# p'w_in of four batches made in one packing, on 64-row tiles, and kept in DRAM

## The chip, the core and the metric

The kernel runs on one core of a Trainium2 chip. The core has TensorE (PE in the profile, with its weight loads as PEld), VectorE (DVE), ScalarE (ACT), GpSimd (POOL) and SyncE (SP, which only issues DMAs here). The metric is the device time of one launch in microseconds (us).

## The reference

Two attentions in a row, and a feed-forward network (FFN) on top, for 8 batches of 8 heads, 576 tokens, head size 64, with 32 packed queries p:

```python
p_packed = sm_attn(p, k, v)                 # 32 rows a head
out = sm_attn(q, p_packed, p_packed)        # 576 rows a head
x = out.transpose(0, 2, 1, 3).reshape(4608, 512)
h = x @ w_in                                # 512 -> 2048
g = np.maximum(h, 0) + alpha * np.minimum(h, 0)
return g @ w_out                            # 2048 -> 512
```

sm_attn(a, k, v) is softmax(a kᵀ / 8) v. Inputs are float32 (w_in and w_out come as 64-bit floats).

## The kernel before, in words

**No x is made.** The second attention's weights a (576 x 32 a head) are multiplied with p'w_in, where p' is p_packed: for a batch, h = sum over heads of a · (p' w_in). p'w_in has 8 heads x 32 = 256 rows and 2048 columns a batch. Heads go in pairs: four pairs (pr), each of 128 rows of w_in.

**Two-part numbers.** Nearly every product is made from a rounded high part and the rest (hi and lo, `fp32r` in the profile), in three matmuls: hi·hi, lo·hi, hi·lo. A split is an ACT copy (hi) and a subtraction on DVE or POOL (lo).

**Stages, by the names in the profile.** `attention(b, tp)` does half a batch (two pairs): scores of p with k (L216, L217; evacuated by L219 and L220), softmax (L280 to L302), its transposes (L328, evacuated and split by L332, L334), v split (L308, L309, into the single buffer vs), the pack matmuls (L350; L358, L359), p' transposed (L375) and stored in two parts (L384, L385; POOL copies it to pt, L409). Then the scores of q with p' (L216, L217 again, with p as weights), and the softmax over 32 (L453 to L470), which leaves a_h and a_l. `packed_w` makes p'w_in of two batches: per column block j of 512 and pair pr, a unit, it reads a split tile of w_in from DRAM (w_split, L582), makes three matmuls of 128x512 with the p' of both batches as weights (L610 to L612) into one PSUM buffer of the two called ps_m, and copies it into pw by ACT (L615, once a batch). The FFN goes by half batches k (0 to 15) and 16 blocks f of 128 hidden columns: `first(k, f)` splits 256 columns of pw (`split_pw`, ACT L626, POOL L628), makes six matmuls of 288 columns (L652 to L654), and applies the activation (L658, L659) and the split (L664, L665); `second(k, f)` adds to four output accumulators in twelve matmuls (L682 to L684). A pair (k, f) is called a step here; steps are numbered 0 to 255 in the order of the list `order`. Batches 2 and 3 are steps 64 to 127, batches 4 and 5 128 to 191, batches 6 and 7 192 to 255.

**What sets the order.** The loop at the program's end writes the FFN step by step and advances the generators in `plan` (attention, packing) by one piece a step, from a given step on. A scheduler then orders each engine's instructions by its own model of time; each engine does its own in that order. All DMAs but two are issued by SP, in one order, each waiting for what it needs; the landings are counted on eight semaphores in turn, and a DMA first waits for the last one on its own semaphore. Before, attention of batches 2g, 2g+1 and their packing stand among the FFN steps of the two batches ahead of them.

**Buffers the change meets.** ps_m has 2 PSUM buffers, `win` (tiles of w_in) 3, `pwp` (pw) 8 of [128, 2, 512], `pt` one tile.

Of the kernel before, what the change touches and what calls it, by code (L numbers as in the profile page):

```python
# [28 lines left out]
def pack_attention_ffn_kernel(  # L29
# [20 lines left out]
    nc = tc.nc  # L50
# [43 lines left out]
    pt = const.tile([P, NP, 2, 2, 64], F32R, name="pt")  # L94
# [134 lines left out]
    def attention(b, tp, exact=False):  # L229
# [92 lines left out]
        for t0 in range(0, KT, 3):  # L322
# [10 lines left out]
            if not exact:  # L333
                nc.vector.tensor_tensor(  # L334
                    out=aT[:, ks, :, 1, :], in0=psq, in1=fv(aT[:, ks, :, 0, :]), op=ALU.subtract
                )
        q0 = load_x(qT, b, pr0)
        yield
        c = sm.tile([P, 2, P], F32, name="c", tag="c", bufs=2)

# [19 lines left out]

        pack(0, vs)
        vs = split_v(1)
        q1 = load_x(qT, b, pr1)
        yield
        pack(1, vs)
        q0 = split(q0)
# [9 lines left out]
        for r in range(2):  # L376
            rs, cs = slice(r * 64, r * 64 + 64), slice(r * N, r * N + N)
            if b == 0:
                for i, pr in enumerate(prs):
                    nc.scalar.copy(out=pt0[rs, pr, pr % 2, cs], in_=ppv[rs, i, cs])  # L380
            elif exact:
                nc.scalar.copy(out=ptf[rs, ts, b, cs], in_=ppv[rs, :, cs])
            else:
                nc.scalar.copy(out=p2[rs, ts, 0, cs], in_=ppv[rs, :, cs])  # L384
                nc.vector.tensor_tensor(  # L385
                    out=p2[rs, ts, 1, cs], in0=ppv[rs, :, cs], in1=fv(p2[rs, ts, 0, cs]),
                    op=ALU.subtract,
                )
        if exact:
            def split_pt():  # L390
                if b > 0:
                    nc.gpsimd.tensor_copy(out=pt[:, ts, 0, b, :], in_=ptf[:, ts, b])
                    nc.gpsimd.tensor_tensor(
                        out=pt[:, ts, 1, b, :], in0=ptf[:, ts, b], in1=fv(pt[:, ts, 0, b, :]),
                        op=ALU.subtract,
                    )
                    return
                for pr in prs:
                    nc.gpsimd.tensor_copy(out=pt[:, pr, 0, 0, :], in_=pt0[:, pr, pr % 2])
                    nc.gpsimd.tensor_tensor(  # L400
                        out=pt[:, pr, 1, 0, :], in0=pt0[:, pr, pr % 2], in1=fv(pt[:, pr, 0, 0, :]),
                        op=ALU.subtract,
                    )

            if b > 0:
                split_pt()
        else:
            for pr in prs:
                nc.gpsimd.tensor_copy(out=pt[:, pr, :, b % 2, :], in_=fv(p2[:, pr]))  # L409
        done.update(("p", b, pr) for pr in prs)  # L410
        owner.update({(pr, b % 2): b for pr in prs})
        q1 = split(q1)
        yield
        s2 = [] if b == 0 else wk.tile([P, S], F32, name="s2", tag="w")
# [203 lines left out]
            yield  # L618


    def split_pw(k, h):
# [4 lines left out]
        nc.scalar.copy(out=th, in_=src)  # L626
        low = nc.vector if k < 4 else nc.gpsimd
        low.tensor_tensor(out=tl, in0=src, in1=fv(th), op=ALU.subtract)  # L628
        pj[k, h] = (th, tl)

    def first(k, f):
        tok = slice((k % 2) * HS, (k % 2) * HS + HS)
        assert all(("a", k, tp) in done for tp in range(2)), ("a", k)
        assert k < 2 and ("wf", f) in done or all(("w", k // 2, f // 4, pr) in done for pr in range(4)), ("w", k, f)
        ps = ps_h.tile([P, 512], F32, name="ps_h", tag="h")
        if k < 2 * XF:
            th, a_f = pw[k // 2, f // 4], result[k // 2]
            fs = slice((f % 4) * P, (f % 4) * P + P)
            for i in range(2):
                nc.tensor.matmul(  # L640
                    ps[:, :HS], th[:, i, fs], a_f[:, i, tok], start=(i == 0), stop=(i == 1)
                )
        else:
            a_h, a_l = result[k // 2]
            key = (k, f // 2)
            if key not in pj:
                split_pw(*key)
            th, tl = pj[key]
            fs = slice((f % 2) * P, (f % 2) * P + P)
            for i in range(2):  # L650
                hi, lo = (i == 0), (i == 1)
                nc.tensor.matmul(ps[:, :HS], th[:, i, fs], a_h[:, i, tok], start=hi, stop=False)  # L652
                nc.tensor.matmul(ps[:, :HS], th[:, i, fs], a_l[:, i, tok], start=False, stop=False)  # L653
                nc.tensor.matmul(ps[:, :HS], tl[:, i, fs], a_h[:, i, tok], start=False, stop=lo)  # L654
# [3 lines left out]
        nc.scalar.activation(out=neg, in_=x, func=AF.Relu, scale=-1.0)  # L658
        nc.vector.scalar_tensor_tensor(  # L659
            out=x, in0=neg, scalar=nal[:, f : f + 1], in1=x, op0=ALU.mult, op1=ALU.add  # L660
        )
        gh = gp.tile([P, HS], F32R, name="gh", tag="gh", bufs=3)
        gl = gp.tile([P, HS], F32R, name="gl", tag="gl", bufs=3)
        nc.scalar.copy(out=gh, in_=x)  # L664
        nc.vector.tensor_tensor(out=gl, in0=x, in1=fv(gh), op=ALU.subtract)  # L665
        gs[k, f] = (gh, gl)
# [57 lines left out]
    def units(*js):  # L724
        return [(j, pr) for j in js for pr in range(NP)]
# [109 lines left out]
```

## Time and profile before

| | us |
|---|---|
| median of 3 runs | 800.36 (799.27 to 802.3) |
| profiled execution, its time | 800.34 |
| its span, first to last instruction | 798.5 |
| TensorE busy | 766.9 |
| ACT, DVE, POOL busy | 542.7, 501.1, 312.4 |
| first matmul of step 64, 128, 192 | 269.4, 458.2, 639.3 |
| packing matmuls of batches 4, 5 | 416.6 to 454.4 |
| packing matmuls of batches 6, 7 | 593.6 to 633.2 |

Rows of groups read: line, engine, operation, out<-in, shapes, count | busy us, mean ns of one | idle time before them and what ended it. Matmuls overlap, so a matmul's own time (0.3 us) is longer than the distance to the next. Rows of stretches give, for each engine, busy us and the number of instructions, then the granted TensorE clock, the mean busy share of the 16 DMA engines, and GB/s.

### The profile page before, as it was taken

The numbers are of one execution on the slowest core, as the hardware profiler recorded it, in microseconds if no ns is written. First come the engines' busy times: TensorE is split into PE (matmuls) and PEld (weight loads), VectorE is DVE, ScalarE is ACT, GpSimd is POOL, SyncE is SP. The second block draws the span as 40 slices with busy tenths as digits, with TensorE's granted clock in tenths as the row PEclk, the third lists the DMA queues.
The fourth block names the chain that finished last, engine by engine and source line by source line (L and its number), as shares of the span: only waits on it lengthen the run. The fifth ranks groups of instructions, "written<-read, shape, count | busy, mean of one in ns | idle before, by whom it ended". The sixth has DMA issues, their size and how long they took to land.

```text
span 798.5 us, 15192 instructions
## 1 busy us (share of the span) xinstructions
PE 766.9 (96%) x5376; PEld 729.6 (91%) x5376; DVE 501.1 (63%) x1112; ACT 542.7 (68%) x1260; POOL 312.4 (39%) x303
## 2 busy tenths in 40 slices
PE   5789997899999999999999999999999999999997
PEld 4566776799999999999999999999999999999997
DVE  4998998878978445666754365665763344444443
ACT  5778888876667977676768766776768644444443
POOL 2211211344535336675664145756543232222320
PEclk9989999999999999999999999999999999999999
DMA  9977896422234753222226621211017200000000
GB/s 333 291 258 256 268 337 219 129 76 60 90 94 126 252 180 92 76 60 75 64 80 219 214 71 50 89 49 58 1 54 253 68 31 1 31 1 31 1 31 30
DMA packets 58459, 93.79 MB, mean 117 GB/s; under 512 B 5136, under 2 KB 36880, under 8 KB 58384
## 3 DMA queue, kind: packets, MB, share of 16 engines
q1 hardware_dynamic: 58096, 92.75, 36.0%
q8 instruction: 42, 0.69, 0.3%
q14 instruction: 33, 0.27, 0.1%
q10 hardware_dynamic: 288, 0.07, 0.0%
HBM read 72.88 MB, written 19.92 MB: 116 GB/s over the span
## 4 chain that ended last, share of the span: by engine, by line
PE 78%; DVE 2%; ACT 1%; DMA 1%; issue 0%; ACTq 0%; DVEq 0%
PE acc L682 15%; PE acc L683 15%; PE acc L684 15%; PE ps_h L652 7%; PE ps_h L653 7%; PE ps_h L654 7%; PE ps_h L640 2%; PE ps_m L350 2%; PE ps_m L216 1%; PE ps_m L217 1%; PE ps_m L610 1%; PE ps_m L612 1%; PE ps_m L611 1%; PE ps_m L328 1%; DMA w<-w_split 1%; PE ps_m L375 0%
## 5 line engine op out<-in xcount | busy, mean ns | idle before, releaser
L682 PE MATMUL acc<-gh,wo 128*128 128x288 f32 x1024 | 287.2, 300 | 3.7 <-ACT gh L664 3.7
L683 PE MATMUL acc<-gh,wo 128*128 128x288 f32 x1024 | 282.8, 295 | 0.0
L659 DVE SCALAR_TENSOR_TENSOR ps_h<-neg,nal,ps_h 128x288 f32<-128x288 f32 x256 | 132.0, 517 | 141.0 <-ACT neg L658 140.1
L628 POOL TENSOR_TENSOR pwl<-pw,pwh 128x512 fp32r<-128x512 f32 x96 | 124.3, 1295 | 213.4 <-ACT pwh L626 192.1
L684 PE MATMUL acc<-gl,wo 128*128 128x288 f32 x1024 | 202.3, 300 | 0.0
L682 PEld LDWEIGHTS acc<-gh,wo 128*128 128x128 f32 x1024 | 192.3, 188 | 9.7 <-ACT gh L664 6.5
L683 PEld LDWEIGHTS acc<-gh,wo 128*128 128x128 f32 x1024 | 192.3, 188 | 1.7 <-issue 0.2
L665 DVE TENSOR_TENSOR gl<-ps_h,gh 128x288 fp32r<-128x288 f32 x256 | 115.8, 454 | 81.1 <-ACT gh L664 78.6
L684 PEld LDWEIGHTS acc<-gl,wo 128*128 128x128 f32 x1024 | 158.4, 188 | 4.2 <-issue 0.9
L664 ACT CAST gh<-ps_h 128x288 fp32r<-128x288 f32 x256 | 102.1, 400 | 79.5 <-DVE ps_h L659 77.8
L658 ACT ACTIVATE neg<-ps_h 128x288 f32<-128x288 f32 x256 | 104.7, 410 | 45.1 <-PE ps_h L654 39.3
L652 PE MATMUL ps_h<-a_h,pwh 128*128 128x288 f32 x448 | 133.2, 297 | 0.8 <-DVE gl L665 0.8
L653 PE MATMUL ps_h<-a_l,pwh 128*128 128x288 f32 x448 | 132.1, 295 | 0.0
L654 PE MATMUL ps_h<-a_h,pwl 128*128 128x288 f32 x448 | 132.1, 295 | 0.0
L626 ACT CAST pwh<-pw 128x512 fp32r<-128x512 f32 x112 | 69.4, 620 | 62.2 <-PE ps_h L653 60.9
L180 POOL TENSOR_TENSOR xl<-xraw,xh 128x576 fp32r<-128x576 f32 x48 | 69.0, 1440 | 93.0 <-ACT xh L179 88.8
L652 PEld LDWEIGHTS ps_h<-a_h,pwh 128*128 128x128 f32 x448 | 84.1, 188 | 2.0 <-DVE gl L665 1.6
L653 PEld LDWEIGHTS ps_h<-a_l,pwh 128*128 128x128 f32 x448 | 84.2, 188 | 0.4
L654 PEld LDWEIGHTS ps_h<-a_h,pwl 128*128 128x128 f32 x448 | 84.1, 188 | 0.2
L615 ACT COPY pw<-ps_m 64x512 f32<-64x512 f32 x120 | 69.6, 580 | 7.8 <-PE ps_m L612 5.7
L309 POOL TENSOR_TENSOR vs<-vraw,vs 128x640 fp32r<-128x640 f32 x24 | 38.1, 1586 | 32.4 <-ACT vs L308 32.3
L219 ACT COPY lo<-ps_m 64x288 f32<-64x288 f32 x96 | 37.2, 396 | 7.5 <-PE ps_m L217 5.8
(133 smaller groups left out, 996.2 us busy)
## 6 DMA issues: line engine op xcount, KB each, us to landing
w<-w_split SPq DMA_DIRECT2D x48, 512.0 KB, 4.2
xraw<-in_kT SPq DMA_DIRECT2D x32, 288.0 KB, 2.9
xraw<-in_qT SPq DMA_DIRECT2D x32, 288.0 KB, 2.9
outT<-ot SPq DMA_DIRECT2D x64, 144.0 KB, 2.3
vraw<-in_v SPq DMA_DIRECT2D x32, 256.0 KB, 2.9
wraw<-in_w_in SPq DMA_DIRECT2D x16, 512.0 KB, 4.8
wraw<-in_w_out SPq DMA_DIRECT2D x16, 512.0 KB, 4.9
w_split<-w SPq DMA_DIRECT2D x16, 512.0 KB, 4.1
```

The costliest lines, as they stand in the source:

```text
L615: nc.scalar.copy(out=pw[b, j][ro : ro + 64, pr // 2, :], in_=ps[i * 64 : i * 64 + 64, :])
L628: low.tensor_tensor(out=tl, in0=src, in1=fv(th), op=ALU.subtract)
L652: nc.tensor.matmul(ps[:, :HS], th[:, i, fs], a_h[:, i, tok], start=hi, stop=False)
L653: nc.tensor.matmul(ps[:, :HS], th[:, i, fs], a_l[:, i, tok], start=False, stop=False)
L654: nc.tensor.matmul(ps[:, :HS], tl[:, i, fs], a_h[:, i, tok], start=False, stop=lo)
L658: nc.scalar.activation(out=neg, in_=x, func=AF.Relu, scale=-1.0)
L659: nc.vector.scalar_tensor_tensor(out=x, in0=neg, scalar=nal[:, f : f + 1], in1=x, op0=ALU.mult, op1=ALU.add)
L664: nc.scalar.copy(out=gh, in_=x)
L665: nc.vector.tensor_tensor(out=gl, in0=x, in1=fv(gh), op=ALU.subtract)
L682: nc.tensor.matmul(acc[o][:, :HS], wo_t[f][:, 0, os_], gh, start=begin, stop=False)
L683: nc.tensor.matmul(acc[o][:, :HS], wo_t[f][:, 1, os_], gh, start=False, stop=False)
L684: nc.tensor.matmul(acc[o][:, :HS], wo_t[f][:, 0, os_], gl, start=False, stop=end)
```

## The change

For batches 0 to 3 nothing changes. For batches 4 to 7:

- Attention of all four is planned among steps 64 to 127 (`AG` has eight starts). For batches 6 and 7 it stops after p' (`HELD`), and the q part (load, split, scores) follows from steps 132 to 148 on.
- p' is kept in a tile `pt4`, which takes the place of `pt` and holds all four batches: each pair's tile has 128 columns, 32 rows of p' x 4 batches, and its upper 64 partitions belong to one head, its lower 64 to the other. POOL copies a held batch's p' back into `p2` for the scores of q.
- `packed_w_four` has 16 units as before, once in place of twice. A unit makes six matmuls with 64 rows and 128 columns of weights (three a head), each head into a ps_m buffer of its own. ACT copies each buffer into hi, DVE subtracts into lo, and two DMAs of 512 KB write hi and lo to a DRAM tensor `pw_four` (two-part p'w_in of four batches).
- `fetch_pw` reads the two parts for (k, j) back, 512 KB each, four steps ahead, into the same eight pwp tiles. The splits of pw (L626, L628) fall away for batches 4 to 7.

```diff
+    pw_four = [dram.tile([2, 2, P, 4, 512], F32, name=f"pw_four{j}") for j in range(NJ)]
...
+            while clock[0] < HELD[b][tp]:
+                yield
...
+    def packed_w_four(units):
+        def get(j, pr):
+            w = win.tile([P, 2, 512], F32R, name="w", tag="w")
+            nc.sync.dma_start(out=fv(w), in_=w_split[j, pr])
+            return w
...
+            ps = [ps_m.tile([P, 512], F32, name="ps_m", tag="m") for r in range(2)]
+            for n, (pp, wp) in enumerate(((0, 0), (1, 0), (0, 1))):
+                for r in range(2):
+                    rs = slice(r * 64, r * 64 + 64)
+                    nc.tensor.matmul(
+                        ps[r], pt_four()[rs, pr, pp], w[rs, wp], start=(n == 0), stop=(n == 2)
+                    )
+            hi, lo = (pwp.tile([P, 2, 512], F32R, name=n, tag="pw") for n in ("hi4", "lo4"))
+            for r in range(2):
+                nc.scalar.copy(out=hi[:, r], in_=ps[r])
+                nc.vector.tensor_tensor(out=lo[:, r], in0=ps[r], in1=fv(hi[:, r]), op=ALU.subtract)
+            for part, t in enumerate((hi, lo)):
+                to = pw_four[j][part, pr // 2, pr % 2 * 64 : pr % 2 * 64 + 64]
+                nc.sync.dma_start(
+                    out=to.rearrange("(r n) b c -> (n b) r c", r=2), in_=fv(t)
+                )
+            yield
+
+    def fetch_pw(k, j):
...
+        th, tl = (pwp.tile([P, 2, 512], F32R, name=n, tag="pw") for n in ("pwh4", "pwl4"))
+        for part, t in enumerate((th, tl)):
+            nc.sync.dma_start(
+                out=fv(t), in_=pw_four[j][part, :, :, k // 2 % 4].rearrange("t p c -> p t c")
+            )
+        pj[k, j] = (th, tl)
...
+    HELD = {6: (132, 136), 7: (144, 148)}
...
-    AG = (0, 4, 11, 17, 26)
+    AG = (0, 4, 9, 13, 18, 22, 27, 31, 39)
...
-    for g in range(2, B // 2):
-        T = (g - 1) * 4 * NF
-        plan += [(T + AG[n], attention(2 * g + n // 2, n % 2), 1) for n in range(4)]
-        plan += [(T + AG[4], packed_w([2 * g, 2 * g + 1], units(*range(NJ))), 1)]
+    T = 4 * NF
+    plan += [(T + AG[n], attention(4 + n // 2, n % 2), 1) for n in range(8)]
+    plan += [(T + AG[8], packed_w_four(units(*range(NJ))), 1)]
```

How the scheduler's order comes out is seen on TensorE and SP. On TensorE before, a unit of batches 4 and 5 (L610 to L612) stands in the middle of an FFN step of batches 2 and 3 (L684 and L682 to L683 are output matmuls of two steps that follow each other):

```order
L684 MATMUL acc_5801<-gl,wo_542 128x288
L684 MATMUL acc_5802<-gl,wo_542 128x288
L610 MATMUL ps_m<-w,pt 128x512
L611 MATMUL ps_m<-w,pt 128x512
L612 MATMUL ps_m<-w,pt 128x512
L684 MATMUL acc_5803<-gl,wo_542 128x288
L682 MATMUL acc_5800<-gh,wo_634 128x288
L683 MATMUL acc_5800<-gh,wo_634 128x288
```

After, all 96 matmuls of the 16 units (L671; pt_4025 is pt4) stand in one piece between the end of batch 7's p' (L224 and L225 scores, L359 pack, L386 p' transposed, L336 transposes) and the held scores of q (p_113 is p2):

```order
L359 MATMUL ps_m<-vs,aT 128x256 x5
L224 MATMUL ps_m<-xh,s_112 128x288
L225 MATMUL ps_m<-xl,s_112 128x288
L224 MATMUL ps_m<-xh,s_112 128x288
L225 MATMUL ps_m<-xl,s_112 128x288
L386 MATMUL ps_m<-ii,c 128x64 x2
L336 MATMUL ps_m<-ident,s_t 128x128 x5
L359 MATMUL ps_m<-vs,aT 128x256 x10
L386 MATMUL ps_m<-ii,c 128x64 x2
L671 MATMUL ps_m<-w,pt_4025 128x512 x96
L224 MATMUL ps_m<-xh,p_113 128x288
L225 MATMUL ps_m<-xl,p_113 128x288
```

The last output matmul of batches 2 and 3 (step 127) stands 16 rows ahead of L671, before the packs of the last two halves; the first FFN matmul of batch 4 (step 128) stands behind 14 of the held score matmuls. On SP, the first fetch for step 128 (L691) stands behind the writes (L680) of 15 of the 16 units:

```order
L657 DMA w<-w_split 128x1024
L680 DMA pw_four_104<-hi_6377 128x2x512
L680 DMA pw_four_104<-lo_6378 128x2x512
L680 DMA pw_four_104<-hi_6439 128x2x512
L680 DMA pw_four_104<-lo_6440 128x2x512
L680 DMA pw_four_104<-hi_6469 128x2x512
L680 DMA pw_four_104<-lo_6470 128x2x512
L691 DMA pwh_6631<-pw_four_101 128x2x512
L691 DMA pwl_6632<-pw_four_101 128x2x512
L680 DMA pw_four_104<-hi_6511 128x2x512
```

The earlier units have a read of w_split ahead of each pair of writes; the reads of the first three units stand far ahead, among the FFN steps.

More of the change, by code (lines that the diff above doesn't have):

```diff
@@ L93, in pack_attention_ffn_kernel @@
     p2 = const.tile([P, NP, 2, 64], F32R, name="p2")
[L94 removed]
+    pt = const.tile([P, NP, 2, 2, 64], F32R, name="pt", tag="pt")
     nc.gpsimd.memset(s1f, 0.0)
@@ L101, in pack_attention_ffn_kernel, with pt_four @@
     wo_t = {}
+    four = {}
+    def pt_four():
+        if not four:
+            four[0] = const.tile([P, NP, 2, P], F32R, name="pt4", tag="pt")
+        return four[0]
     XF = 1
@@ L336, in attention @@
                 )
-        q0 = load_x(qT, b, pr0)
+        if b not in HELD:
+            q0 = load_x(qT, b, pr0)
         yield
@@ L362, in attention @@
         vs = split_v(1)
-        q1 = load_x(qT, b, pr1)
+        if b not in HELD:
+            q1 = load_x(qT, b, pr1)
         yield
         pack(1, vs)
-        q0 = split(q0)
+        if b not in HELD:
+            q0 = split(q0)
         yield
@@ L383, in attention @@
             else:
[L384 to L388, printed above, removed]
+                if b in HELD:
+                    ph, pl = (pt_four()[rs, ts, part, b % 4 :: 4] for part in range(2))
+                else:
+                    ph, pl = (p2[rs, ts, part, cs] for part in range(2))
+                nc.scalar.copy(out=ph, in_=ppv[rs, :, cs])
+                nc.vector.tensor_tensor(out=pl, in0=ppv[rs, :, cs], in1=fv(ph), op=ALU.subtract)
         if exact:
@@ L406, in attention @@
                 split_pt()
-        else:
+        elif b < 4:
             for pr in prs:
                 nc.gpsimd.tensor_copy(out=pt[:, pr, :, b % 2, :], in_=fv(p2[:, pr]))
+        elif b not in HELD:
+            for r in range(2):
+                rs, cs = slice(r * 64, r * 64 + 64), slice(r * N, r * N + N)
+                for pr in prs:
+                    nc.gpsimd.tensor_copy(out=pt_four()[rs, pr, :, b % 4 :: 4], in_=fv(p2[rs, pr, :, cs]))
         done.update(("p", b, pr) for pr in prs)
         owner.update({(pr, b % 2): b for pr in prs})
+        if b in HELD:
+            while clock[0] < HELD[b][tp]:
+                yield
+            for r in range(2):
+                rs, cs = slice(r * 64, r * 64 + 64), slice(r * N, r * N + N)
+                for pr in prs:
+                    nc.gpsimd.tensor_copy(
+                        out=p2[rs, pr, :, cs], in_=fv(pt_four()[rs, pr, :, b % 4 :: 4])
+                    )
+            q0 = load_x(qT, b, pr0)
+            q1 = load_x(qT, b, pr1)
+            yield
+            q0 = split(q0)
+            yield
         q1 = split(q1)
@@ L618, in packed_w @@
             yield
+    def packed_w_four(units):
[3 more added lines that the diff above has]
+            return w
+        for got in ahead(get, units):
+            if got is None:
+                yield
+                continue
+            (j, pr), w = got
+            assert all(("p", b, pr) in done for b in range(4, 8)), pr
+            done.update(("w", b, j, pr) for b in range(4, 8))
+            ps = [ps_m.tile([P, 512], F32, name="ps_m", tag="m") for r in range(2)]
+            for n, (pp, wp) in enumerate(((0, 0), (1, 0), (0, 1))):
+                for r in range(2):
+                    rs = slice(r * 64, r * 64 + 64)
[3 more added lines that the diff above has]
+            hi, lo = (pwp.tile([P, 2, 512], F32R, name=n, tag="pw") for n in ("hi4", "lo4"))
+            for r in range(2):
+                nc.scalar.copy(out=hi[:, r], in_=ps[r])
[5 more added lines that the diff above has]
+                )
+            yield
+    def fetch_pw(k, j):
+        if (k, j) in pj or j == NJ:
+            return
+        assert all(("w", k // 2, j, pr) in done for pr in range(NP)), ("w", k, j)
+        th, tl = (pwp.tile([P, 2, 512], F32R, name=n, tag="pw") for n in ("pwh4", "pwl4"))
+        for part, t in enumerate((th, tl)):
+            nc.sync.dma_start(
+                out=fv(t), in_=pw_four[j][part, :, :, k // 2 % 4].rearrange("t p c -> p t c")
+            )
+        pj[k, j] = (th, tl)
     def split_pw(k, h):
@@ L644, in first @@
             a_h, a_l = result[k // 2]
-            key = (k, f // 2)
-            if key not in pj:
-                split_pw(*key)
+            if k < 8:
+                key = (k, f // 2)
+                if key not in pj:
+                    split_pw(*key)
+                fs = slice((f % 2) * P, (f % 2) * P + P)
+            else:
+                key = (k, f // 4)
+                fetch_pw(*key)
+                fs = slice((f % 4) * P, (f % 4) * P + P)
             th, tl = pj[key]
-            fs = slice((f % 2) * P, (f % 2) * P + P)
             for i in range(2):
@@ L783, in pack_attention_ffn_kernel @@
     plan += [(A2[4], packed_w([2, 3], units(*range(NJ))), 1)]
-    for g in range(2, B // 2):
-        T = (g - 1) * 4 * NF
-        plan += [(T + AG[n], attention(2 * g + n // 2, n % 2), 1) for n in range(4)]
-        plan += [(T + AG[4], packed_w([2 * g, 2 * g + 1], units(*range(NJ))), 1)]
-    AHEAD = 2
+    T = 4 * NF
+    plan += [(T + AG[n], attention(4 + n // 2, n % 2), 1) for n in range(8)]
+    plan += [(T + AG[8], packed_w_four(units(*range(NJ))), 1)]
+    AHEAD, FETCH = 2, 4
     for i in range(len(order) + AHEAD):
+        clock[0] = i
+        if i + FETCH < len(order) and order[i + FETCH][0] >= 8:
+            k, f = order[i + FETCH]
+            fetch_pw(k, f // 4)
         now = [gen for t, gen, n in plan for _ in range(max(1, -n)) if t <= i and (n < 0 or (i - t) % n == 0)]
```

1 line of the change is left out of this document (added).

## The prediction, made before the changed kernel ran

> **What bounds the kernel now.** I read the page's shares and its chain first, then the stretches by stage, then the places where the change acts.
>
> ```profile
> span 798.5 us, 15192 instructions
> PE 766.9 (96%) x5376; PEld 729.6 (91%) x5376; DVE 501.1 (63%) x1112; ACT 542.7 (68%) x1260; POOL 312.4 (39%) x303
> PE 78%; DVE 2%; ACT 1%; DMA 1%; issue 0%; ACTq 0%; DVEq 0%
> ...
> core 0: us, PE busy (x) PEld busy (x) DVE busy (x) ACT busy (x) POOL busy (x), PEclk, DMA share, GB/s
> 337.40:458.20 120.80, 120.48 (x880) 118.07 (x879) 67.28 (x152) 90.10 (x203) 63.90 (x59) 1.00 0.37 117
> 458.20:639.30 181.10, 181.10 (x1342) 178.88 (x1341) 103.04 (x236) 126.38 (x294) 90.02 (x80) 1.00 0.25 76
> 650.00:700.00 50.00, 50.00 (x380) 50.00 (x379) 21.22 (x44) 22.57 (x55) 12.92 (x10) 1.00 0.04 13
> ```
>
> TensorE is the bound: it is never idle in the two stretches where this change works. 380 matmuls in 50 us make 0.132 us each for the 288-wide ones, weight load included, although one lasts 0.3 us. The other engines have slack. So whatever empties TensorE's queue costs its full length, and nothing saved on ACT or POOL gains anything here.
>
> **Where the orders part.** TensorE's two orders are the same up to five pack matmuls behind the output matmuls of step 84:
>
> ```profile
> 336.27 0.69 PE L684 MATMUL acc<-gl,wo 128*128 128x288 f32 x4
> 336.80 0.76 PE L350 MATMUL ps_m<-vs,aT 128*128 128x256 f32 x5
> 337.39 0.33 PE L375 MATMUL ps_m<-ii,c 128*128 128x64 f32 x2
> 337.53 0.38 PE L682 MATMUL acc<-gh,wo 128*128 128x288 f32 x1
> ...
> 458.19 0.29 PE L652 MATMUL ps_h<-a_h,pwh 128*128 128x288 f32 x1
> ...
> 430.59 0.23 PE ps_m L611
> 430.82 0.23 PE ps_m L612
> ```
>
> So until 337.4 us nothing changes. 458.19 is the first matmul of step 128, that is of batch 4. Five pack matmuls take 0.59 us (0.118 each), two p' transposes 0.14 (0.07 each), and the last two rows, of the chain, price a 512-wide packing matmul at 0.23.
>
> **Before the block.** Counted in the two orders, up to the last output matmul of step 127 the changed kernel has, against the old one's way to 458.19: 48 packing matmuls fewer (48 x 0.23 = 11.0); 22 score matmuls more (2.9), 10 transposes (1.2, priced as the pack's), 20 pack (2.4), 4 p' (0.3) and 17 output matmuls (2.2). That is -2.0, so 456.2 us. ACT gains attention work here and loses 32 pw copies; its 90 us of 120.8 were covered by TensorE and stay so. I add no stall, but 0 to 6 in the range, as more of the attention is now chained.
>
> **The block.** In the order, TensorE then has nothing but this before step 128: transposes, packs, scores and p' of batch 7 (10 T, 20 pack, 8 score, 4 p', some 5 us of work), all 96 new packing matmuls in one piece, and 14 score matmuls of the held halves. TensorE issues in order, and no FFN step is left to fill the gaps. Its length is that of the chains. First the attention tail:
>
> ```profile
> L698 DVE COPY ot<-acc 128x288 f32<-128x288 f32 x24 | 9.9, 449 | 5.3 <-PE acc L684 5.2
> L280 DVE TENSOR_REDUCE nmx<-s_t 128x1 f32<-128x576 f32 x14 | 10.4, 745 | 0.2
> L294 ACT ACTIVATE s_t<-s_t,nmx 128x576 f32<-128x576 f32 x14 | 10.9, 777 | 0.5 <-DVE nmx L281 0.3
> L302 DVE TENSOR_SCALAR s_t<-s_t,den 128x576 f32<-128x576 f32 x12 | 7.1, 590 | 0.2
> L332 ACT CAST aT<-ps_m 128x384 fp32r<-128x384 f32 x12 | 5.8, 482 | 1.5 <-PE ps_m L328 1.4
> L334 DVE TENSOR_TENSOR aT<-ps_m,aT 128x384 fp32r<-128x384 f32 x12 | 6.6, 550 | 1.1 <-ACT aT L332 1.1
> L308 ACT CAST vs<-vraw 128x640 fp32r<-128x640 f32 x24 | 17.7, 737 | 0.0
> L309 POOL TENSOR_TENSOR vs<-vraw,vs 128x640 fp32r<-128x640 f32 x24 | 38.1, 1586 | 32.4 <-ACT vs L308 32.3
> L358 ACT COPY ct<-ps_m 128x128 f32<-128x128 f32 x24 | 6.5, 269 | 6.2 <-PE ps_m L350 5.9
> L219 ACT COPY lo<-ps_m 64x288 f32<-64x288 f32 x96 | 37.2, 396 | 7.5 <-PE ps_m L217 5.8
> L220 DVE TENSOR_TENSOR s_t<-ps_m,lo 64x288 f32<-64x288 f32 x48 | 21.2, 449 | 17.0 <-ACT lo L219 16.5
> L179 ACT CAST xh<-xraw 128x576 fp32r<-128x576 f32 x48 | 32.3, 673 | 5.4 <-PE ps_m L216 3.1 <-issue 1.3 <-DVE wo L142 1.0
> L385 DVE TENSOR_TENSOR p<-ps_m,p 64x64 fp32r<-64x64 f32 x24 | 5.2, 218 | 1.8 <-ACT p L384 1.3
> ```
>
> From the last output matmul: ot copy 0.45, max scaled and exponential 1.1, division 0.9, five transposes with their two-part split 2.4, pack 0.9: 5.8. The second pack waits for scores that stand ahead of it: ct 0.27, vs cast 0.74, lo 0.40, xh 0.67, lo 0.40, add 0.45, pack 0.9: 3.8. The scores of the last half: ct, vs, lo, xh, lo, add and a matmul's 0.3: 3.2. Its softmax: 0.75, 0.2, exponential 0.9, division 0.9, small copies 0.3: 3.0. Transposes and first pack 2.8. Second pack behind the single vs buffer: 0.27 + 0.74 + 1.59 + 0.9 = 3.5. p' and its four small copies: ct 0.27, add 0.3, a matmul's 0.4, 4 x 0.22: 1.9. Sum 24, with hand-overs **25**; bounds 20 (packs hidden) and 30.
>
> Then the packing. A unit fills both ps_m buffers, and each must be copied by ACT and subtracted by DVE before its next use:
>
> ```profile
> L610 PE MATMUL ps_m<-w,pt 128*128 128x512 f32 x56 | 22.4, 399 | 1.5 <-ACT w L141 1.0 <-DMA w<-w_split 0.6
> L626 ACT CAST pwh<-pw 128x512 fp32r<-128x512 f32 x112 | 69.4, 620 | 62.2 <-PE ps_h L653 60.9 <-POOL xl L180 0.9
> L588 DVE TENSOR_TENSOR w<-w,w 128x512 fp32r<-128x512 f32 x8 | 6.3, 789 | 0.4 <-ACT w L587 0.3
> ...
> w<-w_split SPq DMA_DIRECT2D x48, 512.0 KB, 4.2
> w_split<-w SPq DMA_DIRECT2D x16, 512.0 KB, 4.1
> outT<-ot SPq DMA_DIRECT2D x64, 144.0 KB, 2.3
> ...
> 10.00:20.00 10.00, 8.02 (x48) 6.47 (x47) 8.21 (x25) 8.54 (x26) 1.45 (x4) 1.00 1.08 389
> 110.00:120.00 10.00, 10.00 (x63) 8.78 (x63) 9.97 (x23) 9.41 (x19) 0.00 (x0) 1.00 0.99 343
> ```
>
> A buffer's round is 2 x 0.23 + 0.40 for three matmuls, 0.62 for the cast, 0.79 for the subtraction, with hand-overs 2.4 us a unit. But a unit also reads one 512 KB weight tile and writes two of p'w_in (hi, lo): 1.57 MB in 2.4 us would be 655 GB/s, and the fullest stretches of this trace moved 343 (DMA share 0.99) and 389 (1.08). The DMA engines take over as the bound once the ring of eight pw tiles (four units, two tiles each) is full: the copy of unit n+4 waits until unit n's write has landed. The first fetch, which step 128 waits for, stands on SP behind the writes of 15 units. With three weight tiles loaded ahead that is 13 reads + 30 writes + 1 fetch = 44 x 524,288 B = 23.1 MB: 59.3 us at 389 GB/s, 67.3 at 343; I take 63, as neither stretch has this mix. Ahead of it lie 2.2 us until the first write (0.7 + 0.9 + 0.6), behind it some 1.9 to land (2.3 for a 144 KB transfer less its own 0.4). **Packing to step 128: 67**, bounds 43 (16 x 2.4 and a landing) and 104 (16 x 6.5, the round plus an uncovered landing of 4.1, the landing of such a write). Whether two 64-row tiles run at once, or one after the other (six x 0.23 = 1.4 us a unit), then hardly matters; in 11 of the 16 units the order has three matmuls of one half and then three of the other. The 14 held scores and POOL's p2 copies run while the last writes drain.
>
> The Trainium skill, TensorEngine Tiling (Array Packing), section PSUM Bottleneck, says that tiling speeds up TensorE but not the evacuation of PSUM; by that alone the packing would be those 16 x 2.4 us, and it speaks against the change. The Trainium skill, DMA: Bandwidth & Descriptors, section Specifications, gives about 358 GB/s of HBM per core; by it the transfers would take 64.4 us, but the 389 above exceeds it.
>
> **After the block.** Before, 340.3 us lie behind 458.2. Of them go 48 packing matmuls (11.0), 30 score (4.0), 20 transposes (2.4), 40 pack (4.7), 8 p' (0.6), 14 held scores (1.8) and 17 output matmuls (2.2), all done earlier: 313.6. The FFN pipeline has to refill, and the first output matmul waits for four steps behind the first FFN matmuls; in the first 50 us, with TensorE often idle, the granted clock was lower, too:
>
> ```profile
> L658 ACT ACTIVATE neg<-ps_h 128x288 f32<-128x288 f32 x256 | 104.7, 410 | 45.1 <-PE ps_h L654 39.3
> L659 DVE SCALAR_TENSOR_TENSOR ps_h<-neg,nal,ps_h 128x288 f32<-128x288 f32 x256 | 132.0, 517 | 141.0 <-ACT neg L658 140.1
> L664 ACT CAST gh<-ps_h 128x288 fp32r<-128x288 f32 x256 | 102.1, 400 | 79.5 <-DVE ps_h L659 77.8
> L665 DVE TENSOR_TENSOR gl<-ps_h,gh 128x288 fp32r<-128x288 f32 x256 | 115.8, 454 | 81.1 <-ACT gh L664 78.6
> ...
> 0.00:50.00 50.00, 33.83 (x164) 26.80 (x165) 38.59 (x104) 33.23 (x86) 10.73 (x31) 0.90 0.92 305
> ```
>
> Relu to gl is 1.8; two more steps' first matmuls (12 x 0.132 = 1.6) run under part of it, so some 1.4 are lost. A clock that fell in the block would cost the restart 0 to 4; I take 1. **316.** The 64 fetches of 512 KB later are 1.05 MB every four steps (9.5 us), 110 GB/s, three column blocks ahead; covered. POOL's 64 pwl and ACT's casts vanish from a stretch where they cost nothing.
>
> **Sum.** 456.2 + 25 + 67 + 316 = 864.2 us of span. The profiled run took 800.34 with a span of 798.5; adding 1.8 gives **866 us**, against the median 800.36 (8% more).
>
> **Rivals.** (1) The evacuation paces the packing, the DMA engines absorb it: 43 in place of 67, 842 us. For: ring and queue hold several units; against: 655 GB/s. (2) The transfers don't overlap, since SP issues in order and each load stands between two writes that wait: 104, 903 us. Against: the program lets eight transfers be under way, and a load waits for a unit's matmuls alone. (3) Not slower: two 64-row tiles run at once, the 96 matmuls take 48 x 0.23, and the waits hide. The packing's place is the stretch between the two batches' FFN; 11.0 us less is 789. It decides only if tail and packing together last under 27 us (456.2 + 316 + 1.8 = 774), and the tail alone is 25. The Trainium skill, TensorEngine Tiling (Array Packing), section Theoretical Speedup, allows up to 2x for such tiles. (4) The change doesn't do what it says, the new matmuls run at full-array pace: no change of the sum, as above.
>
> **Chances.** Forecast 0.73, (1) 0.12, (2) 0.10, (3) 0.03, the rest 0.02 to something slower still. Range 838 to 890: rival (1) with the tail's low end below, 343 GB/s, a tail of 30 and 6 us of stalls above (889). Faster by over 0.5% 0.02, within 0.5% (what a measurement here tells from nothing) 0.02, slower 0.96.
>
> **What would show it.** Right: TensorE nearly idle for some 90 us from about 456, with DMA share near 1 through its last two thirds; ACT's hi cast and DVE's lo ending the waits for TensorE at first, then the pw_four write ending ACT's; some 314 us from batch 4's first matmul to the end. Wrong: DMA share well under 0.9 in the packing, (1) or (2); FFN matmuls between the packing ones, (3); TensorE waiting before 456, a tail that starts earlier.

## The result, and the profile after

The changed kernel takes **866.17 us** (865.98 to 866.88) against 800.49 us (799.27 to 802.3) in the same comparison: a ratio of 1.082, 95% interval 1.080 to 1.084. The forecast was 866.0.

The page of the changed kernel: span, then TensorE's busy tenths, its granted clock and the DMA share in 40 slices of 21.6 us.

```profile
span 864.4 us, 15205 instructions
PE   6599987999999999999995844899999999999998
PEclk9989999999999999999996555699999999999999
DMA  9978776212237522132313499934344333433310
```

One hole of five slices (5, 8, 4, 4, 8), at or near half clock, with the DMA engines full in its last three; elsewhere TensorE is as busy as before. By stages (for each engine busy us and instructions, then clock, DMA share, GB/s), cut at the end of step 127, the first packing matmul and the first FFN matmul of step 128:

```profile
337.40:456.70 119.30, 119.30 (x911) 119.10 (x910) 78.46 (x186) 87.07 (x209) 80.36 (x84) 1.00 0.25 71
456.70:482.70 26.00, 12.71 (x49) 9.81 (x47) 9.54 (x28) 10.41 (x26) 8.84 (x11) 0.61 0.23 69
482.70:549.30 66.60, 39.12 (x111) 22.16 (x111) 25.22 (x42) 22.27 (x43) 4.69 (x9) 0.50 0.97 368
549.30:705.20 155.90, 155.47 (x1156) 154.92 (x1156) 78.68 (x166) 63.16 (x154) 19.47 (x17) 0.98 0.41 139
705.20:864.40 159.20, 154.92 (x1170) 154.68 (x1168) 66.56 (x139) 54.65 (x139) 0.00 (x0) 1.00 0.32 105
```

So 456.7 + 26.0 + 66.6 + 315.1. The chain of waits through the packing (start, us, what), and the longest waits of the packing in those 66.6 us (who, for whom: us in total, times, longest):

```profile
482.81 2.96 PE ps_m L671 x6
...
488.83 3.05 PE ps_m L671 x6
491.90 6.88 DMA w<-w_split
...
530.16 9.32 DMA w<-w_split
```

```profile
ACT hi L676 <- PE ps_m L671: 41.0, 21, 3.3
DVE lo L677 <- ACT hi L676: 38.1, 21, 3.1
PEld ps_m L671 <- DVE lo L677: 37.1, 19, 3.4
PE ps_m L671 <- DMA w<-w_split: 24.7, 11, 2.7
```

The first three units go at 3.0 us each, the pace of copying and subtracting. Then TensorE waits for weight tiles, from 498 on: the one asked for at 491.9 lands at 498.8, and those on this chain take 7 to 9 us among the writes (4.2 before). From 492.7 on the DMA engines move about 400 GB/s (the first three stretches of 10 us):

```profile
482.70:492.70 10.00, 9.95 (x21) 5.67 (x21) 4.18 (x8) 4.05 (x8) 0.00 (x0) 0.50 0.59 188
492.70:502.70 10.00, 7.19 (x17) 3.90 (x17) 4.57 (x7) 3.42 (x6) 0.00 (x0) 0.50 1.02 398
502.70:512.70 10.00, 4.62 (x18) 2.67 (x18) 2.58 (x4) 2.15 (x4) 0.00 (x0) 0.50 1.04 408
```

### The profile page after: what moved, and what is told of

Its sections match the earlier page's. It is cut to its first block, busy times and chain, and to the rows that moved or that the text cites. A ratio compares the mean times of both kernels' runs of the same rounds, so it can differ in the third digit from the quotient of the medians.

```text
span 864.4 us, 15205 instructions
## 1 busy us (share of the span) xinstructions
PE 791.2 (92%) x5376; PEld 737.9 (85%) x5376; DVE 521.4 (60%) x1144; ACT 494.2 (57%) x1164; POOL 232.1 (27%) x255
## 4 chain that ended last, share of the span: by engine, by line
PE 72%; DMA 4%; DVE 3%; ACT 2%; issue 2%; POOL 1%; SPq 0%; ACTq 0%; POOLq 0%; DVEq 0%
PE acc L762 14%; PE acc L763 14%; PE acc L764 14%; PE ps_h L732 6%; PE ps_h L734 6%; PE ps_h L733 6%; DMA w<-w_split 4%; PE ps_h L715 2%; PE ps_m L671 2%; PE ps_m L359 2%; PE ps_m L224 1%; PE ps_m L225 1%; PE ps_m L336 1%; ACT lo L227 0%; DVE lo L677 0%
## 5 line engine op out<-in xcount | busy, mean ns | idle before, releaser
L764 PE MATMUL acc<-gl,wo 128*128 128x288 f32 x1024 | 196.7, 299 | 0.0
L764 PEld LDWEIGHTS acc<-gl,wo 128*128 128x128 f32 x1024 | 156.3, 188 | 3.5 <-issue 0.9
L671 PE MATMUL ps_m<-w,pt 64*128 64x512 f32 x96 | 33.6, 677 | 24.9 <-DMA w<-w_split 24.7
L703 POOL TENSOR_TENSOR pwl<-pw,pwh 128x512 fp32r<-128x512 f32 x32 | 41.6, 1301 | 40.8 <-ACT pwh L701 40.1
L671 PEld LDWEIGHTS ps_m<-w,pt 64*128 64x128 f32 x96 | 18.5, 314 | 39.4 <-DVE lo L677 37.1
L677 DVE TENSOR_TENSOR lo<-ps_m,hi 128x512 fp32r<-128x512 f32 x32 | 21.1, 688 | 38.1 <-ACT hi L676 38.1
```

Of the source, the lines that this page charges most:

```text
L671: nc.tensor.matmul(ps[r], pt_four()[rs, pr, pp], w[rs, wp], start=(n == 0), stop=(n == 2))
L764: nc.tensor.matmul(acc[o][:, :HS], wo_t[f][:, 0, os_], gl, start=False, stop=end)
```

## Experiments: what paces the packing

My theory at this point: the whole loss is the exposed block, and bytes pace its packing. The rival: ACT, DVE and the half clock pace it. Four kernels change what a unit does after its matmuls; each was run once, and four runs of the changed kernel lie within 0.9 us.

**Lo not written.**

```diff
-            for part, t in enumerate((hi, lo)):
+            for part, t in ((0, hi),):
...
-                out=fv(t), in_=pw_four[j][part, :, :, k // 2 % 4]...
+                out=fv(t), in_=pw_four[j][0, :, :, k // 2 % 4]...
```

> Leaves out: lo is made but not written to DRAM, and hi's region is read in its place, so the low part of p'w_in of batches 4 to 7 is wrong. Theory (the packing is paced by its 1.57 MB a unit through the DMA engines): 13 weight reads, 15 writes and the two fetches of step 128 are 15.7 MB, 43 us at the 368 GB/s of the changed kernel's packing; with 4 us at the ends 47, in place of 66.6, or 16 rounds of 3.0 us (48) and a landing if the evacuation is next in line: about 847 us. Rival (evacuation or the half clock paces the units): nothing they wait for has changed, packing 67, 866 us.

Measured 853.0 us, 6 above the forecast.

**No subtraction.**

```diff
...
-                nc.vector.tensor_tensor(out=lo[:, r], in0=ps[r], in1=fv(hi[:, r]), op=ALU.subtract)
-            for part, t in enumerate((hi, lo)):
+            for part, t in enumerate((hi, hi)):
```

> Leaves out: the DVE subtraction that makes lo; hi is written to both places, so the low part of p'w_in of batches 4 to 7 is wrong. Theory (bytes pace the units): the same bytes go through, packing 66 to 67, 866 us. Rival (evacuation paces): 0.69 us fewer in each buffer's round, 16 x 0.69 = 11 us fewer, 855 us or less.

Measured 865.2 us.

**No writes.**

```diff
-            for part, t in enumerate((hi, lo)):
-                to = pw_four[j][part, ...]
-                nc.sync.dma_start(out=to.rearrange(...), in_=fv(t))
...
-                out=fv(t), in_=pw_four[j][part, :, :, k // 2 % 4]...
+                out=fv(t), in_=w_split[j, k // 2 % 4]
```

> Leaves out: both writes to DRAM; step 128 and later read tiles of w_in in place of p'w_in, so batches 4 to 7 are wrong. Theory: what is left is the evacuation's round, 16 x 2.4 at full clock to 16 x 3.0 at half clock, that is 38 to 48 us with DMA share well under 1: 837 to 848 us. Rival (evacuation at half clock paces already): packing 60 to 67, 860 to 866 us. Rival (transfers wait for each other): 13 loads and the rounds, under 35 us.

Measured 853.4 us, 5 above the range.

**Kept whole.** The edit also writes one tile a unit and brings back the splits for the FFN (not shown).

```diff
-                nc.scalar.copy(out=hi[:, r], in_=ps[r])
-                nc.vector.tensor_tensor(out=lo[:, r], in0=ps[r], in1=fv(hi[:, r]), op=ALU.subtract)
+                if r:
+                    nc.vector.tensor_copy(out=hi[:, r], in_=ps[r])
+                else:
+                    nc.scalar.copy(out=hi[:, r], in_=ps[r])
...
```

> p'w_in of batches 4 to 7 is kept in DRAM whole (fp32, 512 KB a unit, ACT copies one head and DVE the other), read back once a batch and split by ACT and POOL as before. Theory: 13 reads, 15 writes and one fetch are 15.2 MB, 41 us at 368 GB/s; with the ends 45: 844 us. The splits come back to ACT and POOL in a stretch where they had cost nothing: no change there. Rival (evacuation paces): ACT and DVE work side by side, a round of 1.6 + 0.6 us at half clock, 16 x 2.2 = 35, 835 us; with the DMA share well under 0.9.

Measured 849.9 us, 6 above the forecast. The stretch from the first packing matmul to the first FFN matmul of step 128 in each of the four, in this order:

```profile
482.50:534.70 52.20, 49.31 (x101) 27.50 (x100) 23.52 (x36) 20.62 (x37) 1.00 (x3) 0.50 0.90 298
```

```profile
482.40:548.20 65.80, 35.40 (x111) 20.79 (x110) 4.96 (x11) 22.48 (x44) 5.97 (x10) 0.50 0.97 371
```

```profile
485.30:536.00 50.70, 49.30 (x101) 27.49 (x101) 23.13 (x35) 19.69 (x35) 0.00 (x0) 0.50 0.56 191
```

```profile
484.50:530.80 46.30, 34.49 (x107) 20.14 (x106) 12.95 (x21) 12.21 (x24) 1.98 (x3) 0.50 0.93 345
```

Taking away DVE's work with the bytes left changes nothing (65.8 against 66.6). Taking away a third of a unit's bytes shortens it by 14.4 us, and taking away all writes hardly more (50.7): a second floor stands at 48 us, 16 rounds of 3.0. So bytes do pace it, but with only some 15 us between them and the next limit. I had put that limit at 2.4 us a unit. The timeline of the kernel without writes shows the round (start, us, engine, what, idle before):

```profile
500.56 0.93 PEld L671 LDWEIGHTS ps_m<-w,pt 64*128 64x128 f32 x3 [0.79 <-DVE lo L677]
502.24 0.59 ACT L676 CAST hi<-ps_m 128x512 fp32r<-128x512 f32 x1 [1.13 <-PE ps_m L671]
502.86 0.69 DVE L677 TENSOR_TENSOR lo<-ps_m,hi 128x512 fp32r<-128x512 f32 x1 [1.03 <-ACT hi L676]
503.61 0.93 PEld L671 LDWEIGHTS ps_m<-w,pt 64*128 64x128 f32 x3 [0.79 <-DVE lo L677]
```

From the first weight load to the cast, three matmuls take 1.68 us at the granted clock of 0.50, where I had 0.86 at full clock; the cast and the subtraction are shorter than priced (0.59 and 0.69 for 0.62 and 0.79). Keeping p'w_in whole brings 16 us, and the splits that return to ACT and POOL cost little: 317.2 us from step 128 on, against 315.1.

**Alternating halves.** Does it matter in the block whether two 64-row tiles run at once?

```diff
-                    nc.tensor.matmul(
+                    mm = nc.tensor.matmul(
                         ps[r], pt_four()[rs, pr, pp], w[rs, wp], start=(n == 0), stop=(n == 2)
                     )
+                    if n or r:
+                        tc.keep_in_program_order(mm)
```

> The changed kernel with the six matmuls of a unit kept in alternating order (head 0, head 1, head 0, ...), in place of three of one half and then three of the other in most units; everything else as it was. The traces of the runs before show pairs of 64-row matmuls that start 0.004 us apart and 0.33 us after the pair ahead. Theory (bytes pace the packing, not TensorE): a unit's matmuls get shorter, the writes don't: packing 64 to 67 us, 862 to 867 us. Rival (the buffers' round, with three matmuls one after the other in it, still sets part of the pace): the round loses up to 0.5 us at half clock where a pair runs at once, but both buffers must then be free together: 855 to 872 us, with the DMA share below 0.9.

Measured 867.6 us, ratio 1.083 (1.081 to 1.086), with the packing stretch

```profile
482.70:549.00 66.30, 33.81 (x105) 17.82 (x104) 23.73 (x39) 20.40 (x40) 3.97 (x6) 0.50 0.97 369
```

It doesn't: the matmuls' busy time falls from 39.1 to 33.8 us and the stretch stays. But the edit changed less than it seems. In the changed kernel, too, the matmuls of the two halves start in pairs from the seventh unit on, 0.003 to 0.04 us apart, and that in units that stand in the program as three of one half and then three of the other (7, 9, ... 15) as much as in those that alternate (8, 10, ... 16). Only the first six units ran mostly one half after the other.

## Experiments: is the exposed block the whole loss?

If so, a packing that stands among FFN steps should cost no more than before. Attention of batches 4 to 7 was planned 16 to 19 steps earlier, with the changed packing, with the whole one, and with the whole one in alternating order.

```diff
-    AG = (0, 4, 9, 13, 18, 22, 27, 31, 39)
+    AG = (-16, -12, -8, -4, 0, 4, 8, 12, 20)
...
-            four[0] = const.tile([P, NP, 2, P], F32R, name="pt4", tag="pt")
+            four[0] = const.tile([P, NP, P], F32R, name="pt4h", tag="s1f")
+            four[1] = const.tile([P, NP, P], F32R, name="pt4l", tag="ptf")
...
```

> The changed kernel with attention of batches 4 to 7 planned 16 to 19 steps earlier (starts at -16, -12, ... 12, packing at 20, relative to step 64); p' of the four batches lies in the places of two tiles that batches 0 and 1 have left, so that it need not wait for pt. Nothing else differs: same bytes, same matmuls, same PSUM buffers. In the order 75 of the 96 packing matmuls now stand among FFN steps, 21 (3.5 units) behind step 127, and the attention tail is gone. Theory (the loss is the exposed block alone): 3.5 units at 4 us, a landing and the restart, some 20 us, remain of 93 + 5; the half-array matmuls stand in threes, so each costs a full slot and nothing is gained on TensorE: 800 + 20, with 0 to 10 for attention that now crowds the steps before 64: 820 to 830 us. Rival (the round trip through DRAM and the 64-row tiles cost this wherever they stand): 850 us or more.

> Attention early as in the run before, and p'w_in kept whole in DRAM (half the bytes). In the order all 96 packing matmuls stand among FFN steps. Theory: no block is left; 96 matmuls in threes of one half cost what the 96 of the kernel before cost, so 800 us plus 0 to 12 for the crowded attention: 800 to 812 us. Rival (the packing is slower than the FFN that should cover it, and TensorE waits in the middle of the steps): 815 us and more, with idle TensorE between steps 108 and 128.

> As the run before, and the six matmuls of a unit are kept in the order in which they are written (halves alternating), so that two 64-row tiles can run at once. In the order 18 matmuls (3 units) stand behind step 127. Theory: if two tiles run at once a unit takes 3 to 4 slots of 0.23 us in place of 6, 16 x 2.5 x 0.23 = 9 us fewer; 3 units exposed at 3 us and a restart of 5 cost 14: 800 to 815 us; the distance between starts inside a unit tells it apart: 0.23 a pair against 0.23 each. Rival (64-row tiles run one after the other at full pace): no fewer, 810 to 825 us.

Measured 870.0 us (ratio 1.087, 1.085 to 1.088), 869.1 (1.085, 1.084 to 1.087) and 863.4 (1.079, 1.077 to 1.081). **My theory fell**: the block is gone but for 16.7 us, and the time is no shorter. The first of them by stages, from 269.4 (where step 64 began in the kernel before; here it begins at 288.8), cut at 404.0 (step 88 begins), at the end of step 127 and at the first FFN matmul of step 128:

```profile
269.40:404.00 134.60, 110.33 (x636) 96.46 (x637) 68.78 (x164) 93.11 (x216) 81.23 (x108) 0.85 0.42 134
404.00:535.60 131.60, 131.28 (x875) 117.25 (x874) 70.16 (x150) 71.17 (x165) 42.77 (x41) 1.00 0.50 165
535.60:552.30 16.70, 11.13 (x37) 6.71 (x35) 8.87 (x17) 8.60 (x18) 4.75 (x13) 0.66 0.98 351
```

Step 128 begins at 552.3, as late as in the changed kernel (549.3). Step 88 begins at 403.9 in place of 341.9, and TensorE is idle for 24 us of the 134.6 ahead of it, at a mean clock of 0.85 (1.00 between steps 64 and 88 of the changed kernel). What fell behind is the packing of batches 2 and 3, whose matmuls (count, ns min/median/max, first and last start; the line is L641 in the changed kernel, L647 here) share ACT, DVE and the two ps_m buffers with the attention that now stands ahead of it. TensorE's waits just ahead of them end mostly with that attention's work: with s_t 6.0 us, with aT 2.6.

```profile
L641 PE MATMUL ps_m<-w,pt x32: 388/393/499, 94.5 to 297.7; 128*128 128x512 f32 x24, 128*64 128x512 f32 x8
```

```profile
L647 PE MATMUL ps_m<-w,pt x32: 390/420/796, 93.7 to 365.5; 128*128 128x512 f32 x24, 128*64 128x512 f32 x8
```

The last p' matmul of batch 7 starts at 462.9 us in place of 482.4: planned 19 steps (some 45 us) earlier, it gained 20. The second of the three kernels has no exposed block to speak of (step 127 ends at 547.3, step 128 begins at 549.8) and is as slow. Its rival had the time right, but not the reason: between steps 108 and 128 TensorE isn't idle. In the first kernel and the changed one a half of attention takes about 25 to 31 us while FFN steps run (p' at 315, 346, 373, 402, 431 in the changed kernel, at 313, 338, 367, 392, 421 here). That leads to a new theory: **eight halves of attention ahead of step 128 are a cost of their own**, wherever they are put, and the packing is another. Two kernels tell them apart. The first moves 12 of the 16 units behind the start of step 128, each just ahead of the steps that read it, and leaves attention alone; the second has the same packing, but needs the attention of batches 4 and 5 only.

```diff
-    plan += [(T + AG[8], packed_w_four(units(*range(NJ))), 1)]
+    plan += [(T + AG[8], packed_w_four(units(0)), 1)]
+    plan += [(122, packed_w_four(units(1, 2, 3)), 1)]
```

> The changed kernel with only the place of the last 12 packing units altered: the units of the first column block j = 0 stay where they are, those of j = 1 to 3 are planned one a step from step 122, ahead of the steps that read them. In the order 36 of the 96 packing matmuls (6 units) stand before step 128, 60 among the steps 128 to 138. Attention as in the changed kernel. Theory now (two costs: an exposed packing, and attention of four batches that must be done before step 128): the packing's 66.6 us shrink to 6 units at 3 to 4 us and a fetch, 20 to 27, the 10 units under FFN cost their six slots of 0.23, 14, as they stand in threes; the tail of 26 stays: 866 - 66.6 + 24 + 14 = 837, say 830 to 848 us. Rival (time lost in one place comes back in another, as in the early runs, because packing itself can't be covered): 860 us or more.

```diff
-    HELD = {6: (132, 136), 7: (144, 148)}
+    HELD = {}
...
+                    for n in (b % 4, b % 4 + 2):
+                        nc.gpsimd.tensor_copy(out=pt_four()[rs, pr, :, n::4], in_=fv(p2[rs, pr, :, cs]))
...
+    plan += [(2 * T + AG[n], attention(6 + n // 2, n % 2), 1) for n in range(4)]
...
```

> Leaves out: p' of batches 6 and 7 in the packing; the p' of batches 4 and 5 take their columns, so the outputs of batches 6 and 7 are wrong. All matmuls, splits, writes and fetches of the packing stay, and attention of batches 6 and 7 runs at its old place among steps 128 to 191, with nothing held; the packing is staged as in the run before. In the order its 96 matmuls stand in threes among steps 114 to 140. Theory (attention of four batches ahead of step 128 is a cost of its own, and a packing under FFN steps costs no more than before): no tail, no block: 800 plus some 0 to 15 for a restart and waits for w tiles and fetches, that is 800 to 815, at least 25 us below the run before. Rival (64-row tiles, the split at PSUM and the trip through DRAM cost this wherever they stand): within 10 us of the run before.

> As the run before (the same part is left out), with p'w_in whole in DRAM and the six matmuls of a unit in alternating order. This is what the packing of four batches could give if attention were in time. Theory: pairs of 64-row tiles run at once, a unit takes 3 to 4 slots of 0.23 us in place of 6, 7 to 11 us fewer than 801: 788 to 800 us. Rival (tiles don't run at once, or the trip through DRAM stalls the steps that read it): no less than 800 us.

Measured 871.6, 828.3 and 818.0 us, one run each. The attention theory holds, by the difference it named: 43 us between the first two (at least 25 expected). Step 128 begins 48 us earlier in the second (460.3 for 508.5); 26 of that are the attention tail, and most of the rest are the six units that had to wait for batch 7's p' in the first. But all three miss their ranges, by 24, 13 and 18 us: a packing under FFN steps isn't free either. The first, by the stretches from step 127's end (tail, packing to step 128, steps 128 to 159), and its longest waits of TensorE for fetches from 460 to 600:

```profile
456.50:482.50 26.00, 12.69 (x49) 9.77 (x47) 9.51 (x28) 10.41 (x26) 8.80 (x11) 0.60 0.24 69
482.50:508.50 26.00, 17.18 (x38) 9.59 (x37) 8.74 (x14) 7.47 (x14) 0.00 (x0) 0.50 0.81 294
508.50:634.20 125.70, 111.82 (x652) 99.19 (x653) 61.94 (x124) 50.45 (x114) 21.95 (x24) 0.83 0.66 229
```

```profile
PE ps_h L732 <- DMA pwh<-pw_four: 16.0, 4, 7.7
PE ps_h L734 <- DMA pwl<-pw_four: 4.1, 2, 3.1
```

Step 128 came 41 us earlier, as expected, and steps 128 to 159 gave it all back: 125.7 us where the changed kernel takes 79.5. TensorE waits for fetches to land, as each four steps (9.5 us) now need four units and a fetch pair, 7.3 MB, 20 us at 368 GB/s. The first two such groups took 24.2 and 22.7 us, with a DMA share of 0.88 and 0.93, and each ends with a write's landing and then a fetch's on the path (4.5 and 5.8 us, 6.4 and 6.5). So the bytes, and the trip through DRAM behind them, bound the FFN that was to cover them, at a mean clock of 0.83.

With the attention of batches 6 and 7 at its old place (the second kernel), the stretches of steps 112 to 127, 128 to 159 and 160 to 191:

```profile
406.90:460.30 53.40, 53.40 (x342) 45.99 (x341) 31.19 (x61) 28.45 (x65) 17.75 (x22) 1.00 0.68 227
460.30:585.20 124.90, 113.87 (x728) 103.56 (x727) 66.97 (x148) 63.60 (x150) 31.30 (x29) 0.90 0.72 244
585.20:667.30 82.10, 82.10 (x624) 82.10 (x624) 46.99 (x105) 38.83 (x99) 15.04 (x11) 1.00 0.35 116
```

and in the kernel before:

```profile
407.30:458.20 50.90, 50.90 (x350) 48.70 (x350) 21.72 (x47) 40.83 (x85) 18.53 (x17) 1.00 0.60 195
458.20:545.40 87.20, 87.20 (x666) 87.08 (x665) 54.80 (x130) 59.75 (x144) 52.16 (x47) 1.00 0.21 62
545.40:639.30 93.90, 93.90 (x679) 91.80 (x678) 48.24 (x107) 66.63 (x150) 37.86 (x33) 1.00 0.28 90
```

+2.5, +37.7 and -11.8. Part of it is in the matmuls. TensorE's timeline in the second kernel around one set of three packing matmuls, all of one half (start, us, what), and around a set of six, three of one half and then three of the other in the program:

```profile
431.65 0.29 PE L765 MATMUL acc<-gh,wo 128*128 128x288 f32 x1
431.87 0.96 PE L673 MATMUL ps_m<-w,pt 64*128 64x512 f32 x3
432.76 0.40 PE L734 MATMUL ps_h<-a_h,pwh 128*128 128x288 f32 x1
433.00 0.29 PE L735 MATMUL ps_h<-a_l,pwh 128*128 128x288 f32 x1
...
450.81 0.69 PE L766 MATMUL acc<-gl,wo 128*128 128x288 f32 x4
451.43 0.97 PE L673 MATMUL ps_m<-w,pt 64*128 64x512 f32 x6
452.33 0.40 PE L764 MATMUL acc<-gh,wo 128*128 128x288 f32 x1
452.57 0.30 PE L765 MATMUL acc<-gh,wo 128*128 128x288 f32 x1
```

From the FFN matmul ahead to the second one behind are 1.35 us; less their own 2 x 0.132, the set of three costs **1.09 us**. The set of six costs no more, 1.10 (from the fourth matmul of the row at 450.81, 3 x 0.13 later, to 452.57): its matmuls start in pairs, one of each half, 0.01 us apart. In the kernel before, three full-array matmuls cost 0.70 (from the second matmul of the row at 429.93, 0.13 later, to 431.02; the rows of the second and third packing matmul are left out):

```profile
429.93 0.43 PE L684 MATMUL acc<-gl,wo 128*128 128x288 f32 x2
430.20 0.39 PE L610 MATMUL ps_m<-w,pt 128*128 128x512 f32 x1
...
430.89 0.29 PE L682 MATMUL acc<-gh,wo 128*128 128x288 f32 x1
431.02 0.29 PE L683 MATMUL acc<-gh,wo 128*128 128x288 f32 x1
```

So each visit to the 64-row tiles costs some 0.4 us beyond its matmuls. A unit in two sets costs 2.17 us where two full-array units cost 1.39, 12.5 us more over 16 units, as in the early kernel with p'w_in whole, which has 32 sets of three; all six in one visit would save 0.3, some 5 us in all. The kernel here has 17 sets of three and five of six among its 25, so at these costs its sets make only some 6 of the 28 us between it and the one before. TensorE's idle time in steps 128 to 159 is 11.0 us, 7.2 of them until a fetch lands. The clock fell to 0.68 and 0.74 between 500 and 540 us; at the 19.1 and 14.6 us that TensorE was busy there, this is some 10 us (0.32 x 19.1 + 0.26 x 14.6). These are estimates, and the pieces may overlap.

**Two batches at a time** undoes the four-batch part and keeps tiles, splits and DRAM.

```diff
-    HELD = {6: (132, 136), 7: (144, 148)}
+    HELD = {}
...
-                        ps[r], pt_four()[rs, pr, pp], w[rs, wp], start=(n == 0), stop=(n == 2)
+                        ps[r][:64], pt_four()[rs, pr, pp], w[rs, wp], start=(n == 0), stop=(n == 2)
...
+    for g in range(2, B // 2):
+        T = (g - 1) * 4 * NF
...
```

> The four-batch part is undone: batches 4, 5 and then 6, 7 are packed two at a time as in the kernel before (attention at its old places, no held half), still on 64-row tiles (64 columns of weights), split as it leaves PSUM and kept in DRAM. In the order 48 of the 96 matmuls of batches 4 and 5 stand behind step 127, all of 6 and 7 among FFN steps. Theory (the exposed block alone): 8 exposed units of 1.05 MB, at the 3 us of their evacuation 24, a landing and the restart 7, less their own covered time; 12 slots of 0.23 more for each 2 covered units, 24 x 3 x 0.23 = 17: 800 + 31 + 17 = 840 to 850 us, with batches 6 and 7 nearly as before. Rival (the round trip costs this wherever it stands): 866 us or more.

Measured 887.2 us in one run: far above the theory, within the rival's "866 us or more". The exposed block of eight units, and steps 128 to 191 (181.1 us in the kernel before):

```profile
466.50:498.30 31.80, 16.14 (x58) 7.42 (x58) 13.65 (x24) 12.91 (x26) 2.80 (x2) 0.57 0.97 307
498.30:726.15 227.85, 208.01 (x1364) 184.02 (x1365) 120.89 (x259) 106.03 (x252) 46.65 (x53) 0.91 0.56 183
```

The block was as expected (31). But steps 128 to 191, with the packing of batches 6 and 7, which I had at 11 us, take 46.8 us more. Thirty of its 96 matmuls stand in one piece again (615.4 to 629.3), with no FFN between them, and the first FFN matmul behind them waits 4.0 us for a fetch; from 600 to 645 the clock averages under 0.6. The other 66 stand in 14 sets of three, 1.03 us each where the clock is full, and four of six. TensorE is idle for 19.8 us of this stretch, 9.3 of them until a fetch lands. So the time is the rival's, but the run can't tell whether the trip costs this wherever it stands: much of this packing wasn't covered either.

No version here beats the kernel before.

## Why the prediction was right

- **Nothing changes until 337.4; step 127 ends at 456.2**: 456.7, no stall added.
- **Attention tail 25**: 26.0, and piece by piece: 7.1, 4.1, 2.8, 3.2, 3.6, 4.0 and 1.3 us for the seven terms 5.8, 3.8, 3.2, 3.0, 2.8, 3.5 and 1.9. The fifth was mis-added: its own parts, 2.4 and 0.9, make 3.3.
- **Packing 67, bytes as the bound**: 66.6, DMA share 0.97. The runs without lo's write and without the subtraction carry the reason. That the size came out so close is partly luck: 63 us for 23.1 MB are 367 GB/s, a choice between two stretches of the old trace, and the measured mean of 368 is made of about 400, more than either, and of 188 in the first 10 us. The wait was another, too: it is TensorE that waits, for a weight tile behind the writes, and no wait of ACT in the profile is for the ring of pw tiles. Nor was TensorE nearly idle: matmuls were in flight for 51.8 of the 92.6 us, at half clock for most of them.
- **After it 316**: 315.1. That is 1.5 us over the counted 313.6, where I gave the restart 2.4. The first output matmul of step 128 stands 5 us behind the first FFN matmul, near half clock, behind held attention on ACT and DVE; held scores and the first FFN matmuls fill part of that, and how the net comes to 1.5 wasn't worked out.
- **Rival (1), 43 us by the evacuation**: its round was mis-sized; at half clock it is 3.0 us, 48 in all. **Rival (2)**, transfers one after the other: excluded by 398 to 408 GB/s.
- **Rival (3)**, 789 if all hides: its price was wrong. It took full-array pace and perfect pairs, 0.23 a pair. A pair takes 0.33 us at the head of a set, a visit 0.4 more, and even with attention in time and one DMA of 512 KB written a unit in place of two the chip gave 818.
- **"Whether two 64-row tiles run at once hardly matters"**: so in the block (867.6 us alternating), not among FFN steps: of the early kernels with p'w_in whole the alternating one is 5.7 us faster. Most of its units stand as a set of one and a set of five, 0.62 and 1.09 us, the others' as two of three, 1.09 each.
- **The range's upper end, 889**: its named pieces make 866 + 4 + 5 + 6 = 881. Nothing hangs on it.

What the prediction left unsaid is that the block is a symptom: in every version tried here, what was moved away came back, mostly as late FFN steps.

## What to carry to other kernels

An operation that waits for more of its producer moves that producer's whole chain ahead: ask first whether its engines and buffers have room there, since planning it earlier, as here, can push something else back by as much. Steps that read what is being made cover it badly: here the bytes that bound the exposed stretch bound the covered one too. Half-array tiles should be visited rarely and for long, with both halves in one visit.

## What the runs showed of the hardware that was not expected

- **A visit to 64-row tiles costs TensorE some 0.4 us** at full clock beyond its matmuls: one matmul costs 0.62 us, three of one half 1.07 to 1.13 (68 sets in three kernels), where three on the full array cost 0.69 to 0.72 (28 sets). The Trainium skill, TensorEngine Tiling (Array Packing), section Key Properties, says that a change of tiling mode drains TensorE; these figures agree and give the size.
- **Pairs of 64-row tiles do run at once, in either order**: in the alternating early kernel's sets among FFN steps their starts lie 0.000 to 0.014 us apart, at 0.33 us from pair to pair at first and 0.23 later in a set. In four of the five sets of six that stand in the program as three and three (above), the starts lie in pairs as well, 0.01 to 0.02 us apart, and such a set costs the same 1.10 us.
- **The clock stayed at 0.50 with matmuls in flight nearly all the time**: 49.30 of 50.70 us in the kernel without writes (ends of matmuls are modelled; weight loads were busy for 27.49). The Trainium skill, TensorE: Matmul & The Clock Gate, Part 1, has the full clock come back after some 3.4 us of sustained work; that is not what this stretch shows. Whether its short waits between sets or the 64-row tiles hold the clock down wasn't tried; the 75 that stand in sets among the FFN steps of the first early kernel ran at 1.00.
